# Cosformer attention and a gated feed-forward block: other slots for q and v weightings of batches 5 and 6, gate weight sums, k-v products and tiles

## The chip, the cores and the metric

The kernel runs on one core of a Trainium2 chip. The time is what the device needs for one launch, in microseconds (us), from several runs; the smaller the better. One further execution was taken by the profiler and left a trace. Its own time was 315.15 us, of which the span of the program's instructions is 313.4 us.

A core has five instruction streams that run side by side and wait for each other by semaphores: TensorE (PE: matmuls, with their weight loads as PEld), VectorE (DVE), ScalarE (ACT), GpSimd (POOL) and SyncE (SP). In this kernel POOL and SP mostly issue DMA transfers. Each stream is worked off in order: an instruction that waits holds up all that stand behind it on its engine.

## The reference

```python
def _attn_ref(q, k, v):                      # each (8 batches, 8 heads, 576 positions, 64)
    theta = np.pi / 2.0 * pos / S
    phi = lambda x: concat([relu(x) * cos(theta), relu(x) * sin(theta)], axis=-1)
    q_p, k_p = phi(q), phi(k)
    kv = np.einsum('bhsf,bhsd->bhfd', k_p, v)
    z = np.sum(k_p, axis=2)
    num = np.einsum('bhsf,bhfd->bhsd', q_p, kv)
    den = np.einsum('bhsf,bhf->bhs', q_p, z)[..., None] + 1e-06
    return num / den

def _moe_ref(x, w_gate, w_val, w_out):       # x (4608, 512), d_ff 1536
    g = x @ w_gate
    return (silu(g) * (x @ w_val)) @ w_out
```

The attention's output, with the heads side by side, is x: 4608 tokens of 512 features, which go through the gated feed-forward block.

## The kernel before

**Groups and slots.** The 4608 tokens are nine groups of 512, numbered 0 to 8, each of four token tiles of 128. A batch has 576 tokens, so groups and batches don't coincide: tile 13 holds the first tokens of batch 3, tile 22 the first of batch 5, tile 27 the first of batch 6. The feed-forward block of one group is the skeleton of the kernel. Through a group, the attention work for later groups is hung in between at numbered *slots*. A group has 16 (`SLOTS`): slots 0 to 11 stand behind its twelve 128-wide tiles of d_ff, and slots 12 to 15 within its output product. Slot numbers run on: slot s of group tg is 16 tg + s. The order of every engine's stream is the order in which the code emits instructions; no scheduler reorders them. `at(s, f)` puts f in a plan, and `slot(s)` emits what the plan holds for s, in the order of the `at` calls.

**Feed-forward of a group.** In groups 1 to 4 each d_ff tile is `ffn_fc`: four matmuls with the gate weights and four with the value weights (L593), ACT's silu of the first (L599), DVE's product of the two (L604). In groups 5 to 8 (`GATE`) `ffn_by_quarters` takes the gate product by seven products of quarters instead of eight (Strassen's way in Winograd's form; L651), which needs sums of the gate weights and of x. These sums are `gate_weight_sum` (W1 to W4, L626, on DVE, at the slots in `WSUM`) and `x_sum` (L634). The output product goes the same way from group 2 on, in `out_by_quarters` (L825), with evictions and additions on ACT and DVE (L838 to L866) and sums of h and of the output weights (L797, L788). In it, the last product goes into PSUM bank b, which DVE's L866 reads just before.

**Attention of a batch b from 2 on.** `ROW[b]` is (slots of the four q weightings, slot of the q transposes, slots of the four v weightings, slot of the k-v products). The first three are counted from two groups ahead of group b (`p0`), the last from one ahead (`s0`).

- q weighting of one pair of heads (`phi_q`): ACT's relu in place (L277), then DVE's product with the cosine and sine table (L294). For batch 7, `phi_q_part` does it on ACT alone, in 18 parts (L300). The result is in `r_q`, of which there is one buffer, so the next batch's weightings wait until the transposes have read it.
- `qturn_dma`: two DMA transposes from `r_q` to `phit`, issued by SP.
- v weighting (`vmul`, L304, DVE), with the relu of k beside it (L277, ACT).
- `kv_mm`: 72 matmuls (L350), then copies by ACT and DVE (L374).

**Token tiles.** `TILES[tg]` gives the slots of group tg - 1 at which the four tiles of group tg are made. `a_tile2` is the matmuls (L473, with `phit`) and, on DVE, denominator, reciprocal and x (L487, L496, L500); `x_turn` is a DMA transpose by SP (L577) into `xT`, which the feed-forward matmuls read. In gated groups, the DVE work of tiles at certain slots is put behind the next addition (`behind`). The loop over a group's tiles starts at the second tile for group 2.

**Loads.** `load_behind(b)`, one group after the slots of batch b - 1's transposes at slots 1 or 3, is a small copy on POOL (L1037) that reads `phit[b - 1]`, so it waits for these transposes; behind it, POOL issues the loads of k and v of batch b and of q of the next batch. The stores of a group's output are issued by POOL as well (L748), when the output product is nearly done.

**PSUM.** `take` gives out eight banks, the one that was used longest ago first; an instruction that gets a bank waits for its last reader.

Of the kernel before, what the change touches and what calls it, by code (L numbers as in the profile page):

```python
# [18 lines left out]
def kernel(  # L19
# [31 lines left out]
    KH = KC // 2  # L51
    GATE = (5, 6, 7, 8)
    AHEAD = 5
    WSUM = (31, 39, 47, 63)
    ROW = {2: ((16, 16, 17, 17), 18, (20, 21, 21, 22), 8), 3: ((12, 13, 14, 15), 18, (20, 20, 21, 21), 7),
           4: ((12, 12, 13, 14), 15, (15, 16, 17, 18), 5), 5: ((8, 9, 12, 12), 13, (13, 13, 14, 15), 5),
           6: ((6, 8, 9, 12), 13, (13, 13, 14, 15), 3), 7: ([4 + i // 2 for i in range(18)], 13, (12, 13, 14, 15), 3)}
    TILES = {2: (0, 9, 10, 11), 3: (5, 9, 10, 11), 4: (5, 7, 9, 11), 5: (2, 4, 7, 9), 6: (0, 2, 5, 7), 7: (0, 1, 5, 7), 8: (0, 3, 5, 7)}
    LATE = dict(M=44, V=87, O=131, X=26, x=150, v=(190, 250, 120, 150), e=130, a=90, c=170, b=110, k=120)

    consts = ctx.enter_context(tc.tile_pool(name="consts", bufs=1))
# [25 lines left out]
    def take(n, hold=None, fills=False, seeded=False):  # L87

        taken = {x for r in held.values() for x in r}
        if loose[0]:  # L90
            free = [b for b in range(8) if b not in taken]
            if n == 1:
                bs = [min((b for b in free if filled[b] or not seeded), key=lambda b: used[b])]
            else:
                b0 = min((b for b in free if b + 1 in free), key=lambda b: max(used[b:b + 2]))
                bs = [b0, b0 + 1]
            if hold is not None:
                held[hold] = bs
            for b in bs:
                filled[b] = fills or seeded  # L100
            touch(bs)
            return banks[:, bs[0]] if n == 1 else banks[:, bs[0]:bs[0] + 2]
        free = [b for b in range(0, 8, n) if not any(b <= x < b + n for x in taken)
                and (filled[b] or not seeded)]

        b0 = min(free, key=lambda b: (n == 1 and hold is not None and hold[0] == "o" and b ^ 1 not in taken,
                                      sorted(used[b:b + n], reverse=True)))
        if hold is not None:
            held[hold] = range(b0, b0 + n)
        filled[b0:b0 + n] = [fills or seeded] * n  # L110
        touch(range(b0, b0 + n))
        return banks[:, b0] if n == 1 else banks[:, b0:b0 + n]
# [10 lines left out]
    def give_back(hold, late=1):  # L123
        touch(held.pop(hold), late)
# [66 lines left out]
    for j in range(2):  # L191
        t = kvt[:, j]
# [55 lines left out]
    for j in range(2):  # L248
        t = (wgs_sb.rearrange("p n c u x -> p (n c u x)")[:, 0:G * NC * 2 * W].bitcast(BF16).rearrange(
            "p (g c e w) -> p g c e w", g=G, c=NC, e=2) if j else  # L250
            consts.tile([P, G, NC, 2, W], BF16, name=f"v2_{j}"))
# [152 lines left out]
    def copy_op(eng, out, in_):  # L404
        (nc.scalar.copy if eng == "act" else nc.vector.tensor_copy)(out=out, in_=in_)
# [55 lines left out]
    def a_tile2(t, later=False):  # L461

        (b0, c0), (b1, c1) = (divmod(2 * t + r, NC) for r in range(2))
        ps = take(2, ("a2", t))
        rows[0] += LATE["X"]
        if b0 == b1:
            parts = [(slice(0, P), b0, c0, 2)]
        else:
            parts = [(slice(0, SH), b0, c0, 1), (slice(SH, P), b1, c1, 1)]
        for e in range(2):  # L470
            for g in range(G):
                for ms, b, c, n in parts:
                    nc.tensor.matmul(  # L473
                        out=ps[ms, e, g * D1:(g + 1) * D1],
                        lhsT=phit[b][:, e, g, c:c + n].rearrange("p c s -> p (c s)"),
                        rhs=kv2s[b % 2][:, e, g // 2, g % 2], start=True, stop=True,
                    )
        if later:
            behind.append(lambda: (x_of(t, ps), give_back(("a2", t), LATE["x"]), x_turn(t)))
        else:  # L480
            x_of(t, ps)
            give_back(("a2", t), LATE["x"])
# [73 lines left out]
    def xT_of(t):  # L556
        tg, off = divmod(t, GH // 2)
        if tg not in xT:
            xT[tg] = xtp.tile([P, GH // 2, KC, P], FP16, name="xT")
        return xT[tg][:, off]  # L560

    def x_turn_pe(t, ks=slice(0, KC)):
        ps = take(1, ("xt", t, ks.start)).bitcast(FP16).rearrange("p (k x) -> p k x", x=P)
        for kc in range(ks.start, ks.stop):
            nc.tensor.transpose(out=ps[:, kc], in_=st["x", t][:, kc * P:(kc + 1) * P], identity=ident16)
        st["xt", t, ks.start] = ps[:, ks]

    def x_turned(t, eng, ks=slice(0, KC)):
        copy_op(eng, xT_of(t)[:, ks], st.pop(("xt", t, ks.start)))
        give_back(("xt", t, ks.start))  # L570

    def x_turn(t, fast=False):
        if fast:
            x_turn_pe(t)
            x_turned(t, "act")
        else:
            nc.sync.dma_start_transpose(out=xT_of(t), in_=st["x", t])  # L577
# [45 lines left out]
    def gate_weight_sum(n):  # L623
        o, x, y, op = ((W1, A21, A22, ALU.add), (W2, W1, A11, ALU.subtract), (W3, A11, A21, ALU.subtract),
                       (W4, A12, W2, ALU.subtract))[n]
        nc.vector.tensor_tensor(out=o, in0=x, in1=y, op=op)  # L626
# [288 lines left out]
    def at(s, *fns):  # L915
        plan.setdefault(s, []).extend(fns)
# [8 lines left out]
    def turn(t, fast=False):  # L925
        return lambda: x_turn(t, fast)
# [128 lines left out]
    for n in range(4):  # L1055
        at(WSUM[n], lambda n=n: gate_weight_sum(n))
    for tg in GATE:
        for n in range(4):
            at(SLOTS * (tg - 1) + FC + (2, 2, 3, 3)[n], lambda tg=tg, n=(2, 0, 1, 3)[n]: x_sum(tg, n))
    for b in range(2, B):  # L1060
        s0 = SLOTS * (b - 1)
        p0 = s0 - SLOTS
        keng = "dve" if b == 2 else "act"
        phi, turned, weighed, kv_slot = ROW[b]
        if b > 2:
# [16 lines left out]
    for tg in range(2, NTG):  # L1082
        for i in range(tg == 2, OUT):
            t, s = tg * OUT + i, TILES[tg][i]
            later = tg - 1 in GATE and s in (0, 1, 3, 4, 7, 8)
            at(SLOTS * (tg - 1) + s, lambda t=t, later=later: (a_tile2(t, later), None if later else x_turn(t)))
            if t == 10:
                at(SLOTS * (tg - 1) + s, load_3)
# [50 lines left out]
```

## Time and profile before

| what | us |
| --- | --- |
| median of 4 runs (lowest, highest) | 315.61 (314.75, 316.73) |
| the profiled execution | 315.15 |
| its span | 313.4 |
| PE busy | 304.7 |
| DVE busy | 235.3 |
| ACT busy | 153.7 |
| POOL busy | 65.5 |
| group 2: first product | 87.7 |
| group 3: first product | 121.1 |
| group 4: first product | 154.0 |
| group 5: first product | 186.4 |

The profile's page gives each engine's busy time and its share of the span, then the chain of work that ended last, as shares by engine and by line. A row of a timeline has the start in us, the length, the engine, the line, the operation, what it writes and reads, how many instructions were merged in the row, and in brackets the idle time of the engine ahead of it with what ended that. Matmuls are pipelined, so the length of a row on PE overlaps the start of the next one; the distance between starts is what counts. The TensorE clock was granted in full through the span.

### The profile page before, as it was taken

To read this page: it belongs to the slowest core of one execution; us is meant where nothing else is said; L and a number is where in the kernel's file an instruction comes from. 1 tells how busy PE (TensorE), PEld (TensorE's weight loads), DVE (VectorE), ACT (ScalarE), POOL (GpSimd) and SP (SyncE) were. 2 spreads that over 40 slices of the span, in tenths; PEclk is the share of its full clock that TensorE was granted. 3 is DMA by queue.
4 is the path that set the end of the run, shared out by engine and by line. 5 is a ranking of instruction groups with operands and counts; after the bars stand their busy time and mean duration, and the time that the engine had idled before them with its cause. 6 is when DMAs were issued, how large, how long until landed. Compare 5 with 4: busy or idle time off the path is not lost.

```text
span 313.4 us, 6938 instructions
## 1 busy us (share of the span) xinstructions
PE 304.7 (97%) x2768; PEld 197.1 (63%) x2768; DVE 235.3 (75%) x470; ACT 153.7 (49%) x290; POOL 65.5 (21%) x118
## 2 busy tenths in 40 slices
PE   8899999999999999999999999999999999999994
PEld 4587455445444585547645686668666876787683
DVE  7874777697677987589857987788879568955781
ACT  7554555663336355454535364696553254424530
POOL 7764202001420405030403023200400040032000
PEclk9999999999999999999999999999999999999999
DMA  7999998997799799979698949795930051013004
GB/s 262 221 198 197 207 204 129 235 135 100 128 224 121 119 196 151 191 106 174 108 205 133 154 70 176 109 156 75 212 51 17 2 151 36 17 34 103 2 0 135
DMA packets 72976, 41.08 MB, mean 131 GB/s; under 512 B 49904, under 2 KB 69872, under 8 KB 72944
## 3 DMA queue, kind: packets, MB, share of 16 engines
q0 software_dynamic: 24880, 24.91, 45.7%
q1 hardware_dynamic: 47472, 15.21, 31.0%
q10 hardware_dynamic: 592, 0.52, 0.5%
q8 instruction: 21, 0.34, 0.4%
q14 instruction: 11, 0.09, 0.1%
HBM read 37.75 MB, written 9.44 MB: 151 GB/s over the span
## 4 chain that ended last, share of the span: by engine, by line
PE 87%; DVE 6%; ACT 2%; DMA 2%; issue 1%; DVEq 0%; ACTq 0%
PE banks L593 32%; PE banks L825 16%; PE banks L664 13%; PE banks L651 11%; PE banks L766 6%; PE banks L350 3%; DMA xT<-x 2%; PE banks L473 2%; DVE v L304 1%; PE banks L523 1%; DVE x L500 1%; PE banks L454 1%; DVE sums L797 1%; DVE ht L604 1%; DVE ht L669 1%
## 5 line engine op out<-in xcount | busy, mean ns | idle before, releaser
L599 ACT ACTIVATE sg<-banks 128x512 bf16<-128x512 f32 (+2 forms) x68 | 37.2, 547 | 53.8 <-PE banks L593 50.1
L593 PE MATMUL banks<-xT,wg_sb 128*128 128x512 f16 (+2 forms) x272 | 62.0, 354 | 0.6 <-DMA xT<-x 0.6
L593 PE MATMUL banks<-xT,wv_sb 128*128 128x512 f16 (+2 forms) x272 | 62.0, 354 | 0.0
L604 DVE TENSOR_TENSOR ht<-sg,banks 128x512 f16<-128x512 bf16 (+2 forms) x68 | 41.6, 621 | 23.2 <-PE banks L593 16.0
L748 POOL DMA_DIRECT2D out_dram<-ob x56 | 29.4, 533 | 122.1 <-ACT ob L838 117.1
L664 PE MATMUL banks<-xT,wv_sb 128*128 128x512 f16 x192 | 48.6, 379 | 0.0
L593 PEld LDWEIGHTS <-wv_sb 128*128 128x128 f16 x272 | 26.1, 98 | 26.1
L593 PEld LDWEIGHTS <-wg_sb 128*128 128x128 f16 x272 | 24.7, 98 | 22.3 <-issue 0.9
L825 PEld LDWEIGHTS <-ht 128*128 128x128 f16 x336 | 32.7, 98 | 4.8
L669 DVE TENSOR_TENSOR ht<-sg,banks 128x512 f16<-128x512 bf16 x48 | 31.1, 680 | 3.3 <-ACT sg L657 3.3
L664 PEld LDWEIGHTS <-wv_sb 128*128 128x128 f16 x192 | 18.8, 98 | 13.3
L825 PEld LDWEIGHTS <-sums 128*128 128x128 f16 x252 | 24.6, 98 | 3.8 <-issue 0.9
L657 ACT ACTIVATE sg<-banks 128x512 bf16<-128x512 f32 x36 | 20.5, 589 | 11.9 <-PE banks L651 11.9
L766 PE MATMUL banks<-wo_sb,ht 128*128 128x512 f16 x96 | 22.7, 379 | 0.0
L651 PEld LDWEIGHTS <-wgs_sb 128*128 128x128 f16 x192 | 17.9, 98 | 7.7 <-issue 0.9
L500 DVE TENSOR_TENSOR x<-banks,rec 128x512 f16<-128x512 f32 (+1 forms) x32 | 21.6, 674 | 1.3 <-PE banks L454 0.3
L651 PE MATMUL banks<-kvt,wgs_sb 128*128 128x256 f16 x144 | 21.6, 273 | 0.6 <-DVE x L500 0.3
L825 PE MATMUL banks<-wo_sb,ht 128*128 128x256 f16 x168 | 20.6, 273 | 0.0
L304 DVE TENSOR_TENSOR v<-raw_v,tab 128x1152 bf16<-128x1152 bf16 x27 | 19.6, 752 | 0.5 <-ACT raw_v L888 0.5
L825 PE MATMUL banks<-wt_sb,sums 128*128 128x256 f16 x168 | 19.5, 273 | 0.0
L825 PE MATMUL banks<-wt_sb,ht 128*128 128x256 f16 x168 | 19.5, 273 | 0.0
L838 ACT ACTIVATE ob<-banks 128x512 f32<-128x512 f32 x14 | 8.4, 597 | 20.7 <-PE banks L825 20.7
(123 smaller groups left out, 407.9 us busy)
## 6 DMA issues: line engine op xcount, KB each, us to landing
out_dram<-ob POOLq DMA_DIRECT2D x56, 128.0 KB, 5.6
raw_k<-in_k_dram POOLq DMA_DIRECT2D x7, 576.0 KB, 7.4
raw_q<-in_q_dram POOLq DMA_DIRECT2D x6, 576.0 KB, 12.6
raw_v<-in_v_dram POOLq DMA_DIRECT2D x6, 576.0 KB, 10.0
wo_sb<-in_moe_w_out_dram POOLq DMA_DIRECT2D x3, 512.0 KB, 13.7
out_dram<-ob SPq DMA_DIRECT2D x11, 128.0 KB, 5.4
wg_sb<-in_moe_w_gate_dram POOLq DMA_DIRECT2D x5, 256.0 KB, 8.4
wv_sb<-in_moe_w_val_dram POOLq DMA_DIRECT2D x5, 256.0 KB, 9.2
```

The source lines that it names most:

```text
L304: nc.vector.tensor_tensor(out=v2s[b == 1][:, g, :, :, 0:D], in0=(first if b == 0 and g == 0 else {"v": raw_of(b, "v")})["v"][:, g].unsquee ...
L500: nc.vector.tensor_tensor(out=st["x", t].rearrange("p (y e d) -> p e y d", e=2, d=D)[:, :, ys], in0=ps[:, :, 0:2 * J * D1].rearrange("p e ...
L593: nc.tensor.matmul(out=st["f", tg, fc, lo][i], lhsT=(wg_sb, wv_sb)[i][:, kc, fs], rhs=xT[tg][:, ts, kc], start=(kc == 0), stop=(kc == KC - 1))
L599: nc.scalar.activation(out=sg[:, 0:n], in_=st["f", tg, fc, lo][0], func=AF.Silu, scale=DOWN)
L604: nc.vector.tensor_tensor(out=ht[:, fc, r:r + n], in0=st.pop(("s", tg, fc, lo))[:, 0:n], in1=ps[1], op=ALU.mult)
L651: nc.tensor.matmul(out=to[:, i], lhsT=a[:, c, 2 * u + i], rhs=x[:, :, c], start=first and i == 0 and c == 0, stop=c == KH - 1, skip_group_ ...
L657: nc.scalar.activation(out=gates[u, w][:, :, j * HT:(j + 1) * HT], in_=src, func=AF.Silu, scale=DOWN)
L664: nc.tensor.matmul(out=val[u, i, w], lhsT=wv_sb[:, kc, fc * P:(fc + 1) * P], rhs=xT[tg][:, :, kc], start=(kc == 0), stop=(kc == KC - 1))
L669: nc.vector.tensor_tensor(out=ht[:, fc], in0=gates[u, w][:, i], in1=val.pop((u, i, w)), op=ALU.mult)
L748: (queues or (nc.sync, nc.sync))[e].dma_start(out=out_v[idx // NC, idx % NC][:, cols], in_=ob_of(t)[e * SH:(e + 1) * SH, cols])
L766: nc.tensor.matmul(out=o_ps[t], lhsT=ht[:, fc, r:r + P], rhs=wo_sb[:, fc], start=(fc == 0), stop=(fc == FC - 1))
L825: nc.tensor.matmul(out=to[i][:, 0] if len(to) == 2 else to[0][:, i], lhsT=a[:, kc, i * P:(i + 1) * P], rhs=b[:, kc], start=first and kc == ...
```

## The change

The tables of slots get other entries, and `x_turn` gets a second way that an empty table leaves unused.

```diff
-    WSUM = (31, 39, 47, 63)
-    ROW = {2: ((16, 16, 17, 17), 18, (20, 21, 21, 22), 8), 3: ((12, 13, 14, 15), 18, (20, 20, 21, 21), 7),
-           4: ((12, 12, 13, 14), 15, (15, 16, 17, 18), 5), 5: ((8, 9, 12, 12), 13, (13, 13, 14, 15), 5),
-           6: ((6, 8, 9, 12), 13, (13, 13, 14, 15), 3), 7: ([4 + i // 2 for i in range(18)], 13, (12, 13, 14, 15), 3)}
-    TILES = {2: (0, 9, 10, 11), 3: (5, 9, 10, 11), 4: (5, 7, 9, 11), 5: (2, 4, 7, 9), 6: (0, 2, 5, 7), 7: (0, 1, 5, 7), 8: (0, 3, 5, 7)}
+    WSUM = (32, 39, 49, 64)
+    ROW = {2: ([16, 16, 17, 17], 18, (20, 21, 21, 22), 8), 3: ([12, 13, 14, 15], 18, (20, 20, 21, 21), 6), 4: ([12, 12, 12, 14], 15, (15, 16, 17, 18), 5), 5: ([12, 12, 12, 14], 15, (15, 16, 17, 17), 5), 6: ([6, 8, 11, 12], 14, (13, 14, 14, 17), 3), 7: ([4, 4, 5, 5, 6, 6, 7, 7, 8, 8, 9, 9, 10, 10, 11, 11, 12, 12], 15, (12, 13, 14, 15), 3)}
+    TILES = {2: (1, 9, 10, 11), 3: (5, 9, 10, 11), 4: (5, 7, 9, 11), 5: (3, 4, 7, 9), 6: (0, 2, 5, 7), 7: (0, 1, 5, 7), 8: (0, 3, 5, 7)}
+    FASTX = {}
...
     def x_turn(t, fast=False):
-        if fast:
+        if t in FASTX:
+            at(FASTX[t], lambda: (x_turn_pe(t), x_turned(t, "act")))
+        elif fast:
             x_turn_pe(t)
             x_turned(t, "act")
```

In words, entry by entry:

- Gate weight sums: W1 from the last slot of group 1 to the first of group 2 (31 to 32), W3 from the last slot of group 2 to slot 1 of group 3 (47 to 49), W4 from the last slot of group 3 to the first of group 4 (63 to 64). W2 stays at slot 7 of group 2.
- Batch 3: k-v products from slot 7 to slot 6 of group 2.
- Batch 4: third q weighting from slot 13 to slot 12 of group 2.
- Batch 5, in group 3: first two q weightings from slots 8 and 9 to 12, fourth from 12 to 14, transposes from 13 to 15; v weightings from 13, 13, 14, 15 to 15, 16, 17, 17, where 16 and 17 are slots 0 and 1 of group 4.
- Batch 6, in group 4: third q weighting from slot 9 to 11, transposes from 13 to 14; v weightings from 13, 13, 14, 15 to 13, 14, 14, 17 (slot 1 of group 5).
- Batch 7: transposes from slot 13 to 15 of group 5. Its list of q weightings is the same, written out.
- Tiles: tile 20, the first of group 5, from slot 2 to slot 3 of group 4; the first entry of group 2 from 0 to 1.

No instruction is added or taken away. The streams of SP and POOL keep their order; those of PE, DVE and ACT change at the places named.

## What I expected of it

> **What bounds the kernel now.** I read the busy rows first, then the chain of waits, then TensorE's instructions in order of time, because a kernel whose PE is nearly always busy can only get faster where PE stands still.
>
> ```profile
> PE 304.7 (97%) x2768; PEld 197.1 (63%) x2768; DVE 235.3 (75%) x470; ACT 153.7 (49%) x290; POOL 65.5 (21%) x118
> ...
> PE 87%; DVE 6%; ACT 2%; DMA 2%; issue 1%; DVEq 0%; ACTq 0%
> ```
>
> PE is busy 97% of the span and carries 87% of the chain that ended last. The change adds and removes no PE instruction, so all that it can win is PE's stalls. From PE's order of time, the rows with idle time in brackets, and the one row that a later transfer could make late (169.68):
>
> ```profile
> 119.01 1.47 PE L825 MATMUL banks<-wo_sb,sums 128*128 128x256 f16 x12
> 121.08 1.02 PE L593 MATMUL banks<-xT,wg_sb 128*128 128x512 f16 x4 [0.60 <-DMA xT<-x]
> ...
> 152.66 1.47 PE L825 MATMUL banks<-wo_sb,sums 128*128 128x256 f16 x12 [0.53 <-DVE ob L866]
> ...
> 169.68 0.45 PE L473 MATMUL banks<-kv,phit 128*64 128x65 bf16 x16
> ...
> 193.53 0.60 PE L651 MATMUL banks<-kvt,wgs_sb 128*128 128x256 f16 x4 [0.35 <-DVE x L500]
> 195.32 1.25 PE L350 MATMUL banks<-v,raw_k 64*64 64x130 bf16 x72 [0.33 <-DVE ht L669]
> 204.12 0.60 PE L651 MATMUL banks<-kvt,wgs_sb 128*128 128x256 f16 x4 [0.27 <-ACT banks L680]
> ```
>
> A matmul's modelled end overlaps the next one's start, so I size a stall as the distance between two starts less the usual distance of that form (0.216 us at 128x512, 0.109 us at 128x256). Then the stalls ahead of 121.08 and 152.66 are worth **0.76** and **0.69 us**; one of **0.20 us** lies ahead of 119.01; those at 193.53, 195.32 and 204.12 are worth 0.51, 0.40 and 0.43 us. Together 3.0 us behind 60 us: the most that a change of order there can give. The first two are explained by these rows, of the chain around 114 and of DVE's order of time around 150:
>
> ```profile
> 114.25 6.70 DMA xT<-x
> ```
>
> ```profile
> 148.31 0.69 DVE L855 SCALAR_TENSOR_TENSOR banks<-ob,banks 128x512 f32<-128x512 f32 x1 [0.42 <-PE banks L825]
> 148.92 0.42 DVE L797 TENSOR_TENSOR sums<-ht,sums 128x512 f16<-128x512 f16 x1
> 149.25 1.42 DVE L294 TENSOR_TENSOR r_q<-raw_q,tab 128x1152 bf16<-128x1152 bf16 x2
> 150.59 1.42 DVE L304 TENSOR_TENSOR v<-raw_v,tab 128x1152 bf16<-128x1152 bf16 x2
> 151.93 0.68 DVE L866 SCALAR_TENSOR_TENSOR ob<-banks,ob 128x512 f32<-128x512 f32 x1
> ```
>
> PE's last product into bank b must wait for L866, which stands behind two q weightings and two v weightings; it pays 0.67 us for each (1.42 us for two, 0.08 of it tail).
>
> **Part 1, W1 from slot 31 to 32 and k-v of batch 3 from slot 7 to 6 (group 2).** Behind the weight difference at 88.50, DVE did W1 (89.37 to 90.24) and only then the last q weighting of batch 3 (90.24); its DMA transposes were issued at 91.05. With W1 one slot later they go 0.87 us earlier, into a window where the stores of group 1 still land. POOL's copy that waits for them ran at 103.05; behind it stand four loads of 576 KB (raw q, k, v and q, issued 103.54 to 105.81), and the x transposes of tiles 13, 14 and 15 lie in the same DMA engines behind these loads. That is why tile 15's took 6.70 us, where the page's median is 4.0. Loads that begin earlier end earlier. Ends: 0 (landing set by something else) and 0.76 (all of the stall; the start moves 0.87). I take **0.60**, near the upper end, as each link of the chain waits for the one before and only the overlap with the stores takes some back. DVE itself gives nothing here: it is fed by PE at 106.77 and works without a pause to tile 15's x at 114.23 in either order. The k-v products move from behind tile 7's to ahead of them, 1.18 us of PE in both places; the last v weighting they need ends at about 100.56 and its first use is about 100.7, so there is 0.15 us of cover; without it, a tenth or so is lost. W1 is read only in group 5.
>
> **Part 2, q of batch 4, third weighting from slot 13 to 12.** ACT's relu for it now goes ahead of the eviction at 116.40, in 0.88 us of ACT idle time. DVE's third weighting began at 117.60 because it waited for that relu; without the wait it begins at 117.44. L866 (118.28) follows 0.16 earlier: **0.15 of the 0.20 us stall**.
>
> **Part 3, batch 5 in group 3.** The q weightings leave slots 8 and 9 (DVE 140.15 and 142.01, where DVE was behind, but no PE wait followed) and stand at slots 12, 12, 12, 14; all four v weightings leave group 3's end for slots 15, 0, 1, 1. Between L797 at 148.92 and L866 stand now three weightings, not four: 3 x 0.67 in place of 4 x 0.67. L866 starts at 151.26 in place of 151.93 and PE, which is ready at 151.97, goes on at about 151.99: **0.67 us**. The third relu on ACT (147.43 + 3 x 0.63 = 149.3) is done ahead of the eviction at 149.55. What is late next: the fourth weighting stands behind its relu, this behind the eviction at 152.17; so relu 152.67 to 153.34, weighting to 154.1, and L840 begins at 154.1, as before (154.17). In group 4 DVE gets three more v weightings and W4 a slot later, 2.7 us over the first three tiles; it was idle 0.70 and 1.04 us ahead of two of them and for as long again after, and tile 20's move to slot 3 takes its 1.0 us out of the way. The k-v products at 164.94 need the last v weighting at about 160. Free.
>
> But the q weightings feed two DMA transposes on SP, and these are **issued at 154.2, not 150.82**. The later slot numbers for the transposes themselves (15, 14, 15) change nothing: SP's order is the same, and it waits for the data. Who waits: PE at 169.68 (tile 22, the first with tokens of batch 5), then POOL's copy, behind which stand the loads of batch 6 and of q of batch 7. What the transposes take is read from POOL's copies and SP's issues:
>
> ```profile
> 121.14 11.68 SPq L323 DMA_TRANSPOSE phit<-r_q  x2
> ...
> 150.82 9.83 SPq L323 DMA_TRANSPOSE phit<-r_q  x2
> ```
>
> ```profile
> 134.12 0.18 POOL L1037 COPY hold<-phit 1x2 bf16<-1x2 bf16 x1 [10.01 <-DMA phit<-r_q]
> ...
> 165.44 0.18 POOL L1037 COPY hold<-phit 1x2 bf16<-1x2 bf16 x1 [8.03 <-DMA phit<-r_q]
> ...
> 199.61 0.18 POOL L1037 COPY hold<-phit 1x2 bf16<-1x2 bf16 x1 [9.22 <-DMA phit<-r_q]
> ```
>
> From issue to copy: batch 3 12.0 us, batch 4 13.0, batch 5 14.6, batch 6 16.3 (issued 183.27). After the change tile 22 is due at 169.68 - 0.67 = 169.0 (part 1 moves both sides alike). Ends: no stall, and 154.2 + 16.3 - 169.0 = 1.5 us. I take **nothing**: the nearest row is batch 4's, whose transposes too were issued just behind the first stores of their group (119.91; here 153.20), and gives 167.2.
>
> **The rule that speaks against this.** The Trainium skill ("DMA: Bandwidth & Descriptors", section "Queues, rings and completion order") says that each DMA engine takes turns between its queues, packet by packet. By the rule, transposes that lie wholly beside the eight stores of 128 KB pay for these: 12.0 us (batch 3, nearly alone) plus 1.05 MB at some 207 GB/s (the page's fuller slices), 5.1 us, by my estimate: 171.3, a stall of 2.3 us, and the sum would be a loss of 0.9 us. Batch 4's row had all its stores beside it and took 13.0. The row decides; the rule makes the rival below.
>
> **Part 4, batch 6.** Its third q weighting moves from slot 9 to 11, into the 1.44 us in which DVE waited ahead of L855 (181.43). One v weighting and its relu go from slot 15 to slot 1 of group 5, ahead of L699 at 190.79, which becomes 191.46. PE's product at 192.15 waits for L699's end: **+0.04**. DVE had 0.87 us idle ahead of 192.35, which takes the 0.67; the silu of m7 comes 0.67 later and pushes the next ACT work up to 0.6, with the k-v products at 195.32 still waiting for the same L669. Without that cover the cost is 0.6 us. Stalls at 193.53, 195.32 and 204.12 stay.
>
> **Part 5.** Tile 8's entry in group 2's list (0 to 1) isn't read: that loop starts at the second entry. FASTX is empty. W3 at slot 49 runs in DVE gaps of about 0.35 us each between tiles; it delays one gating product by 0.4, and no bank is short. Free.
>
> **Sum** against the profiled execution's own 315.15 us (span 313.4): -0.60 - 0.15 - 0.67 + 0.04 = **-1.38**, or 313.8. That execution lies 0.46 below the median of the runs, 315.61, so the forecast for a median is **314.2**.
>
> **Rivals.**
> - *Half of it (chance 0.22).* Tile 15's transpose lands at the same distance from its x, its queue being set by the volume ahead of it and by the stores. For it: tiles 13 and 14 took as long, though issued earlier. Against: loads and x transposes end together. -0.15 - 0.67 + 0.04: **314.8**.
> - *The gain is given back in group 5 (0.11).* ACT's first q weighting of batch 7 at 199.61 waits for the transposes of batch 6, and ACT then works without a pause to 206; PE's 0.43 us at 204.12 hangs on it. If loads that are 1.7 us later (copy at 167.2 against 165.44) press on these transposes, they land at the old hour, and the 1.4 us go: **315.6**. Against: loads and x transposes would end at about 182.4, the transposes' data began to move after 183.3.
> - *Slower: the transposes of batch 5 are late (0.14).* One mechanism, at 169.0, by the rule above: tile 22 stalls PE from the moment at which they need more than 14.8 us from issue, and the total is a loss from 16.2 on. At 17.1 it is 2.3 - 1.4 = +0.9, and as the loads behind it then run into batch 6's transposes, up to 1.4 more: 316.5 to 317.9, taken as **316.8**. For it: batches 5 and 6 needed 14.6 and 16.3. Against: these were issued ahead of their stores.
> - *More (0.04):* the stalls of 193 to 204 shrink too: 313.5.
>
> The main case has 0.49, with 313.7 to 314.8 as its own range. The range 313.5 to 316.3 leaves out the upper part of the slower case and little below. About 0.5% (1.6 us) is what a measurement of this kernel can tell from no change, so the main case lies at the edge of it: some 0.24 of its 0.49 fall below 314.0. Faster 0.30, same 0.56, slower 0.14.
>
> **What would show it.** Right: no idle time at the first product of group 3; L866 of group 3 behind three weightings and PE's bracket there gone; PE's row of tile 22 without a bracket; POOL's copies near 102.3 and 166.5. Wrong: a bracket "DMA phit<-r_q" on PE at tile 22; the bracket at group 3's start unchanged; a longer one at group 5's L651 behind ACT's L680.

## The result, and the profile after

| | kernel before | changed kernel |
| --- | --- | --- |
| median, us | 315.75 (64 runs) | 314.64 (43 runs) |
| profiled executions, us | 315.15 and 315.35 | 314.50 and 314.65 |
| their spans, us | 313.4 and 313.6 | 312.7 and 312.9 |

The ratio is 0.9966, with a 95% interval from 0.9957 to 0.9975: a gain of 1.1 us (0.8 to 1.4), where 1.4 was forecast. The second profile of each kernel is one of the experiments below. Line numbers in the changed kernel are shifted by one: L593, L651, L825 and L866 are now L594, L652, L826 and L867; L1037 is L1038; lines above `x_turn` go down by one instead (L300 is L299, L473 is L472).

Busy time and chain, from the page of the changed kernel:

```profile
PE 304.6 (97%) x2768; PEld 197.5 (63%) x2768; DVE 234.6 (75%) x470; ACT 153.5 (49%) x290; POOL 65.8 (21%) x118
...
PE 91%; DVE 4%; DMA 2%; ACT 1%; issue 1%; DVEq 0%; ACTq 0%
```

DVE's share of the chain fell from 6% to 4%, PE's rose from 87% to 91%; nobody's busy time changed by more than 0.7 us. TensorE's order of time, changed kernel, the same places as in the prediction:

```profile
118.67 1.47 PE L826 MATMUL banks<-wo_sb,sums 128*128 128x256 f16 x12
120.32 1.02 PE L594 MATMUL banks<-xT,wg_sb 128*128 128x512 f16 x4 [0.18 <-DMA xT<-x]
...
151.23 1.47 PE L826 MATMUL banks<-wo_sb,sums 128*128 128x256 f16 x12
...
168.24 0.51 PE L472 MATMUL banks<-kv,phit 128*64 128x65 bf16 x16
...
192.20 0.60 PE L652 MATMUL banks<-kvt,wgs_sb 128*128 128x256 f16 x4 [0.41 <-DVE x L499]
193.99 1.25 PE L349 MATMUL banks<-v,raw_k 64*64 64x130 bf16 x72 [0.33 <-DVE ht L670]
...
203.41 0.60 PE L652 MATMUL banks<-kvt,wgs_sb 128*128 128x256 f16 x4 [0.86 <-ACT banks L681]
```

The bracket of DVE's L866 is gone (151.23), that of the x transpose is 0.18 in place of 0.60 (120.32), and a bracket that should have stayed grew from 0.27 to 0.86 us (203.41). The gain of two places was in part given back at a third. A group's length, from its first feed-forward product to the next group's, shows it (us, worked out from the starts on PE; all profiles of the study, the experiments' names are explained below):

| kernel | group 2 | group 3 | group 4 | group 5 |
| --- | --- | --- | --- | --- |
| before, two profiles | 33.39, 33.49 | 32.89, 32.88 | 32.45, 32.45 | **32.51, 32.38** |
| changed, two profiles | 32.80, 32.74 | 32.22, 32.22 | 32.48, 32.43 | **33.19, 33.37** |
| W1 alone (e3) | 32.65 | 32.89 | 32.45 | 32.82 |
| batch 5 alone (e5) | 33.24 | 32.22 | 32.46 | **33.41** |
| q of batch 5 early (e1) | 33.04 | 32.20 | 32.43 | **33.87** |
| batch 6 as before (e2) | 34.00 | 32.22 | 32.45 | **33.11** |
| q of batch 5 later (e6) | 33.00 | 32.20 | 32.94 | 33.28 |
| q of batch 6 early (e10) | 32.82 | 32.22 | 32.43 | **31.99** |
| q of batches 5 and 6 early (e7) | 33.27 | 32.20 | 32.43 | 31.99 |
| q of batches 3, 5 and 6 early (e8) | 32.46 | 32.20 | 32.43 | 32.00 |
| tile 25 as well (e9) | 32.46 | 32.20 | 32.43 | 32.06 |
| q of batch 3 early (e11) | 32.45 | 32.22 | 32.43 | 33.20 |

Group 2 gains 0.67, group 3 gains 0.67, group 5 loses 0.83 (means of the two profiles of each). A further 0.2 us lies ahead of group 2, where the orders are the same; group 2 starts anywhere between 87.52 and 88.16 in these fourteen profiles, so this isn't put down to the change. The profiled executions differ by 0.7 us, the timed runs by 1.1; what makes these 0.4 I can't say.

### The profile page after: what moved, and what is told of

The parts are those of the page before. It is cut to its first block, busy times and chain, and to the rows that moved or that the text cites. A ratio compares the mean times of both kernels' runs of the same rounds, so it can differ in the third digit from the quotient of the medians.

```text
span 312.7 us, 6940 instructions
## 1 busy us (share of the span) xinstructions
PE 304.6 (97%) x2768; PEld 197.5 (63%) x2768; DVE 234.6 (75%) x470; ACT 153.5 (49%) x290; POOL 65.8 (21%) x118
## 4 chain that ended last, share of the span: by engine, by line
PE 91%; DVE 4%; DMA 2%; ACT 1%; issue 1%; DVEq 0%; ACTq 0%
PE banks L594 32%; PE banks L826 18%; PE banks L665 13%; PE banks L652 11%; PE banks L767 6%; PE banks L207 3%; PE banks L349 3%; PE banks L472 2%; DMA xT<-x 2%; PE banks L522 1%; DVE x L499 1%; PE banks L453 1%; DVE ht L605 1%; DVE sums L798 1%; DVE ht L670 1%
## 5 line engine op out<-in xcount | busy, mean ns | idle before, releaser
L594 PE MATMUL banks<-xT,wg_sb 128*128 128x512 f16 (+2 forms) x272 | 62.0, 354 | 0.2 <-DMA xT<-x 0.2
L594 PE MATMUL banks<-xT,wv_sb 128*128 128x512 f16 (+2 forms) x272 | 62.0, 354 | 0.0
L594 PEld LDWEIGHTS <-wv_sb 128*128 128x128 f16 x272 | 26.1, 98 | 26.1
L594 PEld LDWEIGHTS <-wg_sb 128*128 128x128 f16 x272 | 24.8, 98 | 21.9 <-issue 0.4
L826 PEld LDWEIGHTS <-ht 128*128 128x128 f16 x336 | 32.7, 98 | 4.9
L826 PEld LDWEIGHTS <-sums 128*128 128x128 f16 x252 | 24.7, 98 | 2.9
L652 PEld LDWEIGHTS <-wgs_sb 128*128 128x128 f16 x192 | 17.8, 98 | 8.3 <-issue 1.5
L652 PE MATMUL banks<-kvt,wgs_sb 128*128 128x256 f16 x144 | 21.6, 273 | 1.3 <-ACT banks L681 0.9
L826 PE MATMUL banks<-wo_sb,ht 128*128 128x256 f16 x168 | 20.6, 273 | 0.0
L826 PE MATMUL banks<-wt_sb,sums 128*128 128x256 f16 x168 | 19.5, 273 | 0.0
L826 PE MATMUL banks<-wt_sb,ht 128*128 128x256 f16 x168 | 19.5, 273 | 0.0
```

The source lines that it names most:

```text
L594: nc.tensor.matmul(out=st["f", tg, fc, lo][i], lhsT=(wg_sb, wv_sb)[i][:, kc, fs], rhs=xT[tg][:, ts, kc], start=(kc == 0), stop=(kc == KC - 1))
L652: nc.tensor.matmul(out=to[:, i], lhsT=a[:, c, 2 * u + i], rhs=x[:, :, c], start=first and i == 0 and c == 0, stop=c == KH - 1, skip_group_ ...
L826: nc.tensor.matmul(out=to[i][:, 0] if len(to) == 2 else to[0][:, i], lhsT=a[:, kc, i * P:(i + 1) * P], rhs=b[:, kc], start=first and kc == ...
```

## The experiments

My first theory of the loss in group 5 was the one that the prediction had named as a rival: late transposes of batch 5, late loads, and these press on the transposes of batch 6. What makes PE wait is seen on ACT. Its first q weighting of batch 7, in the kernel before and, in the second fence, in the changed one:

```profile
199.61 0.91 ACT L300 ACTIVATE r_q<-raw_q,cs_all 128x256 bf16<-128x256 bf16 x2 [1.43 <-DMA xT<-x]
```

```profile
198.89 0.91 ACT L299 ACTIVATE r_q<-raw_q,cs_all 128x256 bf16<-128x256 bf16 x2 [2.04 <-DMA xT<-x]
```

The profile names the x transposes, which landed about when those of batch 6 did; POOL's copy, which waits for batch 6's alone, started at the same moment, 198.89, in the changed kernel:

```profile
168.53 0.77 POOL L1038 COPY hold<-phit 1x2 bf16<-1x2 bf16 x1 [12.03 <-DMA phit<-r_q]
...
198.89 0.18 POOL L1038 COPY hold<-phit 1x2 bf16<-1x2 bf16 x1 [9.89 <-DMA phit<-r_q]
```

ACT stands until they land and starts 13.2 us behind group 5's first product before, 13.9 after (the landing itself is 0.15 us earlier, at 13.0 and 13.7). Then it works off silus and q weightings with no pause until it reaches the copy (L681) that PE waits for.

This end of the chain is exact. In each of the ten profiles in which ACT waits here, group 5 is as long as the start of POOL's copy, counted from group 5's first product, plus 19.32 us, to 0.01 us: starts of 13.06 to 13.50 go with 32.38 to 32.82, starts of 13.79 to 14.55 with 33.11 to 33.87. So the landing of batch 6's transposes sets this group's length, and the question is what makes it late.

### q of batch 5 early again (e1)

```diff
-5: ([12, 12, 12, 14], 15, (15, 16, 17, 17), 5)
+5: ([8, 9, 12, 12], 13, (15, 16, 17, 17), 5)
```

> The changed kernel with the q weightings of batch 5 back in slots 8, 9, 12, 12 of group 3; its v weightings stay late. Theory (the change gives part of its gain back in group 5: late transposes of batch 5 make the loads behind them late, and these press on the transposes of batch 6, which ACT's first weighting of batch 7 waits for): the transposes of batch 5 are issued some 3 us earlier, those of batch 6 land about 0.6 us earlier against PE, and PE's stall near 203 falls from 1.02 back to about 0.43 us. L867 of group 3 stands behind two weightings only, so no stall returns there. Time 0.5 to 0.7 us below the changed kernel, ratio to before about 0.995. Rival (the give-back comes from the v weighting of batch 6 that now stands ahead of the addition in group 5): the stall near 203 stays at 1.0, ratio about 0.9966 as for the change.

Ratio 0.9958 (0.9943 to 0.9973): it holds both forecasts, and is no evidence for either. The trace is clearer. POOL's copies for batches 5 and 6, and PE at the place in question:

```profile
165.32 0.17 POOL L1038 COPY hold<-phit 1x2 bf16<-1x2 bf16 x1 [8.45 <-DMA phit<-r_q]
...
199.88 0.17 POOL L1038 COPY hold<-phit 1x2 bf16<-1x2 bf16 x1 [10.58 <-DMA phit<-r_q]
```

```profile
203.12 0.42 PE L472 MATMUL banks<-kv,phit 128*128 128x65 bf16 x8 [0.70 <-ACT sg L658]
204.40 0.60 PE L652 MATMUL banks<-kvt,wgs_sb 128*128 128x256 f16 x4 [0.86 <-ACT banks L681]
```

The transposes of batch 5 landed early (165.3, as in the kernel before), the loads behind them were early, and the transposes of batch 6 landed later than in any other profile, 14.4 us behind group 5's first product (185.33). Late loads aren't needed for the loss: the first theory falls as the account of it. L867 stood behind two weightings and group 3 stayed at 32.20, as expected.

### Batch 6 as before (e2), W1 alone (e3), batch 5 alone (e5)

```diff
-6: ([6, 8, 11, 12], 14, (13, 14, 14, 17), 3)
+6: ([6, 8, 9, 12], 13, (13, 13, 14, 15), 3)
```

> The changed kernel with all of batch 6's slots as before. Theory: the stall near 203 stays at about 1.0 us, since the transposes of batch 6 still run beside late loads; ratio about 0.9966. Rival: the addition in group 5 no longer stands behind a v weighting, the stall falls to about 0.43, ratio about 0.995.

Ratio 0.9972 (0.9959 to 0.9986), group 5 at 33.11, and the bracket ahead of L652 still 0.86. So the loss doesn't need batch 6's slots; the rival falls by the trace.

```diff
-    WSUM = (31, 39, 47, 63)
+    WSUM = (32, 39, 47, 63)
```

> The kernel before with W1 at slot 32 and nothing else. Theory: the transposes of batch 3 are issued 0.87 us earlier, the loads behind them too, and the stall at group 3's first product falls from 0.76 to about 0.35 us; the stall of 0.69 us in group 3's output product stays. Time 0.4 us lower, ratio about 0.9987. Rival (the stall fell because the k-v products of batch 3 moved): 0.76 stays, ratio 1.000.

Ratio 0.9990 (0.9976 to 1.0004), which can't be told from 1. In the profile the stall at group 3's first product was gone altogether. But batch 6 as before (e2), with the changed kernel's order up to there, had the longest of all:

```profile
121.62 1.02 PE L594 MATMUL banks<-xT,wg_sb 128*128 128x512 f16 x4 [1.39 <-DMA xT<-x]
```

Over the eight profiles with W1 at slot 32 and batch 3's q weightings unmoved, that stall, sized by starts, is 0, 0.28, 0.35, 0.37, 0.54, 0.58, 0.82 and 1.55 us, mean 0.56; over the three with W1 at 31 it is 0.62, 0.76 and 0.87, mean 0.75. The direction fits; the size of part 1 isn't settled by this.

```diff
-5: ((8, 9, 12, 12), 13, (13, 13, 14, 15), 5)
+5: ((12, 12, 12, 14), 15, (15, 16, 17, 17), 5)
...
-5: (2, 4, 7, 9)
+5: (3, 4, 7, 9)
```

> The kernel before with batch 5's slots and tile 20's as in the changed kernel, nothing else. Theory: the stall of 0.69 us in group 3's output product goes, and the stall near 204 grows from 0.43 to about 1.0: the two nearly cancel, ratio 0.9995 to 1.000. Rival (give-back from batch 6): the 0.69 us stay won, ratio about 0.998.

Ratio 0.9983 (0.9965 to 1.0000), which holds both. In the trace group 3 is at 32.22 and group 5 at 33.41: batch 5's slots (with tile 20's) win 0.67 and lose 0.96 in the same profile, without any change to batch 6. These slots are therefore enough for the loss. If it has one cause, then by e1, in which the q weightings were back, it comes with the v weightings, with tile 20, or with the 0.67 us saved. Which, and by what way over 30 us, stays open. Two causes aren't ruled out either: e1 still had batch 6's slots and W4 late, e2 and e5 had late loads, and no run has batch 5's v weightings late alone.

### The cover at tile 22 (e6)

```diff
-5: ([12, 12, 12, 14], 15, (15, 16, 17, 17), 5)
+5: ([12, 12, 14, 15], 15, (15, 16, 17, 17), 5)
```

> The changed kernel with the third and fourth q weighting of batch 5 later still, at slots 14 and 15 of group 3. In the changed kernel the transposes of batch 5 landed at 168.39 and tile 22's products began at 168.24 with a tenth of a us of waiting. Theory (the cover is used up): issued about 0.7 to 1.3 us later they stall PE at tile 22 for about as long, and the time is 0.5 to 1.2 us above the changed kernel's, ratio 0.998 to 1.000. Rival (there is slack, the transposes end when the stores end, whenever they were issued): no bracket on PE at tile 22, ratio 0.9966.

TensorE at tile 22:

```profile
168.90 0.35 PE L472 MATMUL banks<-kv,phit 128*64 128x65 bf16 x9
169.55 0.32 PE L472 MATMUL banks<-kv,phit 128*64 128x65 bf16 x7 [0.31 <-DMA phit<-r_q]
```

The tile's products alternate between batch 4 and batch 5, eight with the first half of the heads and then eight with the second; each half needs one of the two transposes. The first half runs, and one product of batch 4; the next one waits for the second transpose of batch 5. It is the bracket that the prediction had named as the sign of its slower case. Group 4 grew by 0.5 us to 32.94 and the ratio is 0.9979 (0.9966 to 0.9991). The changed kernel stands just at the edge, where the prediction gave it 1.8 us of cover.

### The transposes of batch 6 issued earlier (e7, e8, e10)

```diff
-5: ([12, 12, 12, 14], 15, (15, 16, 17, 17), 5), 6: ([6, 8, 11, 12], 14, (13, 14, 14, 17), 3)
+5: ([8, 9, 12, 12], 13, (15, 16, 17, 17), 5), 6: ([6, 8, 11, 11], 14, (13, 14, 14, 17), 3)
```

> The changed kernel with the q weightings of batch 5 at slots 8, 9, 12, 12 as before, and the last q weighting of batch 6 a slot earlier, at 11. My first theory of group 5's stall (late loads press on the transposes of batch 6) has lost its support: with early loads these landed 14.4 us after group 5's first product, against 13.7 in the changed kernel. Second theory (what decides is when these transposes are issued, and chance in how they share with the eight stores): issued some 2 us earlier they land 11 to 12.5 us after group 5's first product, ACT does not wait for them, and PE's stall near 203 falls below 0.3 us; ratio 0.994 to 0.995. Rival (they end when the stores end): they land at 13 to 14.4 as in all kernels so far, and the ratio is as with q of batch 5 early alone, 0.9958.

Ratio **0.9929** (0.9910 to 0.9947). The first transpose was issued 5.6 us ahead of group 5's first product, not 3.1, and both had landed 7.3 us behind it, not 13.7: more than expected. Group 5 took 31.99.

> The changed kernel with the last q weighting of batch 6 at slot 11, q of batch 5 left late. Theory (what counts is that the transposes of batch 6 are ahead of the stores of group 4): they land 7 to 9 us after group 5's first product though the loads behind batch 5 end late, PE's stalls near 203 (1.2 us together in the changed kernel) go, ratio 0.992 to 0.994. Rival (late loads hold them up after all): they land at 13 or later and the ratio stays at 0.9966.

The edit is batch 6's part of the one above, alone. Ratio **0.9922** (0.9896 to 0.9949). SP's issue of batch 6's transposes (both as one row, then the second alone), POOL with the stores of group 4 and the copy, then ACT's first q weighting of batch 7, then TensorE at the old stall:

```profile
179.79 8.47 SPq L322 DMA_TRANSPOSE phit<-r_q  x2
...
184.64 3.62 SPq L322 DMA_TRANSPOSE phit<-r_q  x1
```

```profile
184.88 4.20 POOL L749 DMA_DIRECT2D out_dram<-ob  x8 [13.68 <-ACT ob L839]
193.99 0.17 POOL L1038 COPY hold<-phit 1x2 bf16<-1x2 bf16 x1 [4.91 <-DMA phit<-r_q]
```

```profile
196.82 0.90 ACT L299 ACTIVATE r_q<-raw_q,cs_all 128x256 bf16<-128x256 bf16 x2
```

```profile
202.02 0.42 PE L472 MATMUL banks<-kv,phit 128*128 128x65 bf16 x8
202.28 0.60 PE L652 MATMUL banks<-kvt,wgs_sb 128*128 128x256 f16 x4
```

Issued at 179.79 and not at 181.89, two us earlier, they land near 193.8 and not 198.7, nearly five us earlier; ACT doesn't wait, and no bracket is left on PE. Here q of batch 5 is late and so are the loads behind it, and it doesn't matter: the second blow to the first theory. By 184.64 both transposes are being issued, and the eight stores begin at 184.88. In the changed kernel the second transpose is issued after the stores have begun, 185.46 against 184.80:

```profile
184.80 4.20 POOL L749 DMA_DIRECT2D out_dram<-ob  x8 [13.25 <-ACT ob L839]
...
185.46 6.40 SPq L322 DMA_TRANSPOSE phit<-r_q  x1
```

The run with q of batch 5 later (e6) bears on this too: there the second transpose of batch 6 was issued at 187.27, counted from group 5's first product 0.7 us later than in the changed kernel, and the pair landed only 0.1 us later. There, behind the start of the stores, a later issue cost hardly anything; ahead of it, 0.9 us earlier for the second and 2.2 for the first won 5.0.

One slot of one weighting is worth about 0.4% against the changed kernel (0.9922 from six runs, against 0.9966; the intervals don't overlap). The weighting fits into DVE's idle time ahead of L856.

```diff
-3: ([12, 13, 14, 15], 18, (20, 20, 21, 21), 6)
+3: ([12, 13, 14, 14], 18, (20, 20, 21, 21), 6)
```

> As the run before, and the last q weighting of batch 3 at slot 14 of group 1 in place of 15. Theory: the transposes of batch 3 are issued near 88, some 2 us ahead of the changed kernel, the four loads behind them too, and tile 15's x transpose no longer stalls group 3's first product (0.35 us in the changed kernel, 0 to 1.55 in its relatives); 0.3 to 0.8 us below the run before, ratio 0.992 to 0.994. Rival (loads of batch 3 and the stores of group 1 fill the engines until 93, so an earlier issue gains nothing): the stall stays.

The edit goes on top of the one of e7. Ratio **0.9914** (0.9897 to 0.9930), 313.27 us: level with e9 below, and better than both kernels. The stall at group 3's first product, 0.82 us in e7, is gone.

### q of batch 3 early alone (e11), tile 25 (e9)

> The changed kernel with the last q weighting of batch 3 at slot 14 of group 1. Theory: the stall at group 3's first product (0.35 us in the changed kernel's profile, 0 to 1.55 in kernels that have the same order there) goes, 0.2 to 0.7 us, ratio 0.9945 to 0.996. Rival (its disappearance with q of three batches early was chance): a stall of 0.3 us or more, ratio 0.9966.

The edit is batch 3's part of e8, alone. Ratio 0.9955 (0.9938 to 0.9973), which can't be told from the changed kernel's. In the profile there is no stall at group 3's first product, as in the two others with this order: 0 in three of three. All fourteen profiles sort themselves by the start of POOL's copy for batch 3 (L1038), counted from group 2's first product: at 12.4 to 13.95 us the stall is 0 (three profiles), at 14.6 to 14.85 it is 0 to 0.37 (four), at 15.0 to 15.2 it is 0.54 to 1.55 (four), and at 15.36 to 15.43, with W1 at slot 31, 0.62 to 0.87 (three). So the chain of part 1 (weighting, transposes, copy, loads, tile 15's x) is real. With W1 at slot 32 the transposes are always issued 0.87 us earlier, but land only 0.2 to 0.8 us earlier: the changed kernel moves the head of the chain too little to be sure of the end.

```diff
-6: (0, 2, 5, 7)
+6: (0, 1, 5, 7)
...
-6: ([6, 8, 11, 11], 14, (13, 14, 14, 17), 3)
+6: ([6, 8, 11, 11], 14, (13, 13, 14, 15), 3)
```

> As the kernel with q of batches 3, 5 and 6 early, and group 6's second tile (tile 25) at slot 1 of group 5 in place of 2, with batch 6's v weightings at slots 13, 13, 14, 15 of group 4 as before. Left of PE's stalls in group 5 were 0.57 us, which waits for tile 25's x, and 0.49 us ahead of the k-v products; group 6, whose second tile is at slot 1, has neither. Theory: both go, 0.5 to 0.9 us, ratio 0.988 to 0.990. Rival: the additions on DVE, which then come behind two tiles' x, are late instead and the ratio stays at 0.991.

The edit goes on top of the one of e8. Ratio 0.9913 (0.9889 to 0.9938), nothing won on e8. The stall of 0.57 us went and another came: the second half of tile 25's products now waits for tile 24's x, whose bank it gets. The stall ahead of the k-v products stayed.

```profile
188.63 0.29 PE L472 MATMUL banks<-kv,phit 128*128 128x65 bf16 x4
189.38 0.29 PE L472 MATMUL banks<-kv,phit 128*128 128x65 bf16 x4 [0.46 <-DVE x L499]
```

### Both kernels once more (r1, r2)

> The kernel before once more, for a second profile. Theory (the stalls that end on transposes vary between executions of one kernel): the stall at group 3's first product differs from 0.76 and the one near 204 from 0.43 by several tenths of a us, while the stall of 0.69 us ahead of the last product of group 3's output, which an order on DVE makes, is the same to 0.02. Rival: all stalls repeat, and the differences between kernels are theirs.

> The changed kernel once more, for a second profile. Theory: its stalls near 203, 1.2 us together in the first profile, are again well above the 0.4 to 0.6 of the two profiles of the kernel before, while the stall at group 3's first product differs from 0.35. Rival (chance): the stalls near 203 are 0.4 to 0.6 here.

Before: the stall at group 3's first product is 0.87 in place of 0.76, the order-made one 0.690 in place of 0.692, group 5 32.38 in place of 32.51: the two stalls that end on transposes moved by a tenth, not by several as expected. Changed: 0.28 in place of 0.35, group 5 33.37 in place of 33.19. So the loss in group 5 isn't chance of one execution: three profiles with batch 5's v weightings in group 3 lie at 32.38 to 32.82, seven with them late, and batch 6's transposes issued where they were, at 33.11 to 33.87.

## Why the prediction was right, and where not

- **Part 3, DVE's L866: right to 0.02 us.** Forecast 0.67, group 3 shorter by 0.67 in every kernel with the new order. DVE's rows are as forecast, three weightings and then the addition; PE doesn't wait:

```profile
148.49 2.09 DVE L293 TENSOR_TENSOR r_q<-raw_q,tab 128x1152 bf16<-128x1152 bf16 x3
150.50 0.68 DVE L867 SCALAR_TENSOR_TENSOR ob<-banks,ob 128x512 f32<-128x512 f32 x1
```

- **Part 2: right to 0.02 us.** 0.15 forecast; the stall went from 0.20 to 0.03 in every profile with the new slot.
- **Part 1:** 0.60 forecast; about 0.50 between the two profiles of each kernel, and 0.19 between the means of eight and three profiles above, with a spread that is wider than either. The mechanism was right, the number lucky as much as good. The cover of the k-v products held: no idle time ahead of them.
- **What the transposes of batch 5 take: wrong.** Issued when forecast (153.52; 154.2 less the 0.7 won by then). I took batch 4's 13.0 us as the nearest row because its transposes too stood just behind the first stores. They took 15.0, near the 14.6 that the batch itself had needed. The cover of 1.8 us at tile 22 was none. It cost nothing in the changed kernel, by luck: e6 shows that it is used up. The estimate from the Trainium skill's rule of turns between queues ("DMA: Bandwidth & Descriptors", section "Queues, rings and completion order"), 17.1 us, was too long, the row too short; the measured 15.0 decides. The prediction took the rows of batches 5 and 6 as issued ahead of their stores. That is so for the first transpose of each pair only: the second of batch 6, for one, began behind the first store (186.18).

```profile
186.78 5.61 SPq L323 DMA_TRANSPOSE phit<-r_q  x1
```

- **"Stalls at 193.53, 195.32 and 204.12 stay": the step that failed.** The first two did: 0.57 against 0.51, and 0.49 in both kernels (the prediction's 0.40 for the second is 0.49 by its own way of sizing). The third, with the gap at the tile's products just before it, grew from 0.5 to 1.3 us, since batch 6's transposes landed 13.7 us (13.9 in the second profile) behind group 5's first product in place of 13.0 (12.9). With it the group lost 0.83 us. The prediction had counted a longer bracket there among its signs of being wrong. Its main case took the landing of a transfer that it didn't move as fixed; why it came later stays open. The rival "given back in group 5" had the place and the end of the chain right (ACT's wait for these transposes), and its cause isn't borne out: e1 and e10 part the landing from the loads.
- **Part 4, +0.04:** the stall at 192.20 grew by 0.06, but by 0.07 in e2 as well, where batch 6's slots are as before; so this isn't the v weighting's price, and none was seen. Part 5: free.

The sum by groups is -0.67 - 0.67 + 0.83 = -0.5, and -0.7 with what lies ahead of group 2, where 1.4 was forecast; the timed 1.1 us lie between. Parts 1 to 3 won 1.3 of their 1.4 us in the profiles. The likeliest case had its direction and its main terms; a term of the opposite sign was missing, and that the timed gain still lies within 0.3 us of the forecast is in part luck. Its interval, 0.6 us from end to end, is narrower than the 1.6 us that the prediction thought a measurement of this kernel could tell from no change.

## What to carry to other kernels

When PE is busy throughout, list its stalls with what ends each, and then ask of every moved instruction which *transfer* it starts. A transfer that is issued a little late can land later by much more, here 5 us for 2: try to issue it ahead of the next burst of stores, not beside it. When two lengths seem to belong together, such as a landing and a group, take their difference in every profile: where it is constant, the chain between them is settled. A stall that ends on DVE's order repeated here to 0.02 us in every profile and can be summed; one that ends on a landing needs several profiles before it is worth a number.

## What was not expected of the hardware

Counted from group 5's first product, the two transposes of batch 6 were issued 2.2 us (e10) and 2.5 us (e7) earlier than in the changed kernel, and landed 5.0 and 6.4 us earlier, with the same eight stores of 128 KB behind or beside them. The sum of the traffic was the same, so it isn't what counted. With e6, in which a later issue behind the start of the stores cost 0.1 us, this speaks for the order of issue against the stores; no run moves the stores themselves. And the stall at group 3's first product, which ends on a transpose behind four loads, lay between 0.28 and 1.55 us in the seven profiles of kernels with the same order up to there.
